# PSUM as one ring of four two-bank tiles, and attention visits of three score tiles

## The chip, the cores and the metric

The kernel runs on one core of a Trainium2 chip. The metric is the device time of the program in microseconds; the median of several runs is given, and every ratio is against runs of the kernel before made on the same chip in the same rounds. All runs of this study are of the same (fast) state. A profile is of one execution only, and its first 110 us vary most from run to run. The span of a profile is 1.8 us shorter than the time of the same execution (446.4 against 448.2 us for the kernel before).

## The reference

Sigmoid attention over 8 batches, 12 heads, 448 positions and 64 channels, followed by a gated feed-forward block (3584 tokens, 768 to 1536 and back).

```python
def _attn_ref(q, k, v):
    S = q.shape[2]
    scores = (1.0 / np.sqrt(q.shape[-1])) * np.matmul(q, k.transpose(0, 1, 3, 2)) - np.log(S)
    return np.matmul(1.0 / (1.0 + np.exp(-scores)), v).astype(np.float32)

def _moe_ref(x, w_gate, w_val, w_out):
    g = x @ w_gate
    silu = g * (1.0 / (1.0 + np.exp(-g)))
    return (silu * (x @ w_val) @ w_out).astype(np.float32)
# x = attention output as (B*S, H*D) = (3584, 768); w_gate, w_val 768 x 1536; w_out 1536 x 768
```

## The kernel before

TensorE, the matmul engine, carries the kernel, and its program order is fixed by hand. Feed-forward units stand one after the other (a unit is a gate and a value product for 128 hidden columns; an output unit is 128 output rows in two halves), and *visits* of attention are put between them. A visit computes score tiles (four matmuls on 64 x 64 quarters of the array side by side, 128 x 896 in PSUM, the buffer that matmuls write into), and some visits also hold the PV product (28 such matmuls) of a group of four heads. The feed-forward matmuls use the array as one piece of 128 x 128, so every visit changes the shape of the array and changes it back. ScalarE turns a score tile into probabilities (the sigmoid), and VectorE does most of the other reading of PSUM. The first batch's attention runs alone at the start.

The kernel divides PSUM by banks (in this code, stretches of 512 FP32 columns) and uses eight. The scores have two tiles of two banks, and all else shares four tiles of one bank. A tile is handed out again when its readers are done. Which tile is next, and all waits, follow from the order in which the kernel issues its instructions.

```python
psA = ctx.enter_context(tc.tile_pool(name="psA", bufs=2, space=bass.MemoryType.PSUM))   # scores
psG = ctx.enter_context(tc.tile_pool(name="psG", bufs=4, space=bass.MemoryType.PSUM))   # all else
# ...
def trans_pe(n, which):                      # q or k, transposed on TensorE
    t = q16.pop((n, which))
    ps = psG.tile([128, C, 128], BF16, tag="G", name="ps_tr")
    for c in range(C):
        nc.tensor.transpose(out=ps[:, c, :], in_=t[:, c].rearrange("p h d -> p (h d)"), identity=idn)
    d = qkT.tile([128, C, 128], BF16, tag=f"T{which}", name=f"T{which}_{n}")
    nc.vector.tensor_copy(out=d, in_=ps)
# ...
def ffn1(b, f, gate):                        # one half-unit: gate or value
    ps = psG.tile([128, S], FP32, tag="G", name="ps_g" if gate else "ps_vl")
    # ... six matmuls into ps
    if gate:
        s16 = tmp.tile([128, S], FP16, tag="s16", name="s16")
        nc.scalar.activation(out=s16, in_=ps, func=SIGM)
        t1 = tmp.tile([128, S], FP16, tag="t1", name="t1")
        nc.vector.tensor_tensor(out=t1, in0=ps, in1=s16, op=MULT)
    # ... value: hT = ps * HSC * t1 on VectorE

def ffn2(b, m, half):                        # one output half-unit
    # ...
    o = psG.tile([128, hw], FP32, tag="G", name="ps_o")
    # ... twelve matmuls into o, then one VectorE read of o into osb
# ...
visits = [tiles[i:i + 2] for i in range(0, len(tiles), 2)]

def attn_step(group, pvs):
    scs = [(n, c, qk_tile(n, c)) for n, c in group]
    for n in pvs:
        pv(n)
    for n, c, sc in scs:
        sig_tile(n, c, sc)
```

Of the kernel before, what the change touches and what calls it, by code (L numbers as in the profile page):

```python
# [17 lines left out]
def kernel(  # L18
# [28 lines left out]
    psA = ctx.enter_context(tc.tile_pool(name="psA", bufs=2, space=bass.MemoryType.PSUM))  # L47
    psG = ctx.enter_context(tc.tile_pool(name="psG", bufs=4, space=bass.MemoryType.PSUM))
# [67 lines left out]
    def trans_pe(n, which):  # L116
        t = q16.pop((n, which))
        ps = psG.tile([128, C, 128], BF16, tag="G", name="ps_tr")
        for c in range(C):
            nc.tensor.transpose(  # L120
                out=ps[:, c, :], in_=t[:, c].rearrange("p h d -> p (h d)"), identity=idn
            )
        d = qkT.tile([128, C, 128], BF16, tag=f"T{which}", name=f"T{which}_{n}")
        nc.vector.tensor_copy(out=d, in_=ps)  # L124
        qT[(n, which)] = d
# [5 lines left out]
    def qk_tile(n, c):  # L131
        sc = psA.tile([128, 2, 512], FP32, tag="A", name="ps_sc")
# [18 lines left out]
    def pv(n):  # L151
        b, j = divmod(n, NJ)
        P = [psG.tile([128, S], FP32, tag="G", name=f"ps_pv{w}") for w in range(2)]
        vt = v16.pop(n)
        for c in range(C):
            pt = pts.pop((n, c))
            for h2 in range(2):
                for w in range(2):
                    r = slice(w * 64, w * 64 + 64)
                    nc.tensor.matmul(  # L160
                        out=P[w][h2 * 64:(h2 + 1) * 64, :],
# [5 lines left out]
        for h2 in range(2):  # L167
            x = xtp.tile([128, S], FP16, tag="xT", name=f"xT_{b}_{2 * j + h2}")
            for w in range(2):
                nc.vector.tensor_copy(  # L170
                    out=x[w * 64:(w + 1) * 64, :], in_=P[w][h2 * 64:(h2 + 1) * 64, :]
                )
            xT[(b, 2 * j + h2)] = x
# [5 lines left out]
    gcur = {}  # L179

    def ffn1(b, f, gate):
        ps = psG.tile([128, S], FP32, tag="G", name="ps_g" if gate else "ps_vl")
        w = (wg16 if gate else wv16)[f // FW]
        cs = slice((f % FW) * 128, (f % FW) * 128 + 128)
        for pr in range(NP):
            nc.tensor.matmul(  # L186
                out=ps, lhsT=w[:, pr, cs], rhs=xT[(b, pr)], start=(pr == 0), stop=(pr == NP - 1)
            )
        if gate:
            s16 = tmp.tile([128, S], FP16, tag="s16", name="s16")  # L190
            nc.scalar.activation(out=s16, in_=ps, func=SIGM)  # L191
            t1 = tmp.tile([128, S], FP16, tag="t1", name="t1")
            nc.vector.tensor_tensor(out=t1, in0=ps, in1=s16, op=MULT)  # L193
            gcur[0] = t1
        else:
            if b % 2 == 0:
                hT[(b // 2, f)] = htp.tile([128, 2, S], FP16, tag="hT", name=f"hT_{b // 2}_{f}")
            nc.vector.scalar_tensor_tensor(  # L198
                out=hT[(b // 2, f)][:, b % 2, :], in0=ps, scalar=HSC, in1=gcur[0], op0=MULT, op1=MULT
            )  # L200

    osb_cur = {}

    def ffn2(b, m, half):
        hw = DM // 2
        if half == 0:
            osb_cur[0] = osp.tile([128, DM], FP32, tag="osb", name="osb")
        osb = osb_cur[0]
        o = psG.tile([128, hw], FP32, tag="G", name="ps_o")
        for f in range(NF):  # L210
            h = hT[(b // 2, f)].rearrange("p b s -> p (b s)")
            lhsT = h[:, m * 128:(m + 1) * 128]
            nc.tensor.matmul(  # L213
                out=o,
                lhsT=lhsT,
                rhs=wo16[f // FW][:, f % FW, half * hw:(half + 1) * hw],
                start=(f == 0),
                stop=(f == NF - 1),
            )
        nc.vector.tensor_scalar(  # L220
# [175 lines left out]
```

## Time and profile before

| | before |
|---|---|
| time | 449.93 us, median of 3 runs (449.58 to 449.96) |
| span of the profile | 446.4 us |
| TensorE busy | 420.9 us, 94% |
| VectorE, ScalarE busy | 49%, 47% |

This is the waits view of the kernel before, TensorE alone (who waited for whom: us in total, times, longest):

```profile
PE ps_sc L137 <- ACT pt L148: 7.2, 10, 2.1
PE ps_tr L120 <- DVE c L108: 4.7, 1, 4.7
PE ps_tr L120 <- ACT c L106: 1.8, 1, 1.8
PE ps_sc L137 <- DVE T L124: 1.6, 2, 0.9
PE ps_g L186 <- DVE xT L170: 1.4, 2, 0.9
...
```

All but 0.5 us of this lies in the first 40 us. After that a single gate product waits, 0.5 us for its input xT.

### The profile page before, as it was taken

The numbers are of one execution on the slowest core, as the hardware profiler recorded it, in microseconds if no ns is written. First come the engines' busy times: TensorE is split into PE (matmuls) and PEld (weight loads), VectorE is DVE, ScalarE is ACT, GpSimd is POOL, SyncE is SP. The second block draws the span as 40 slices with busy tenths as digits, with TensorE's granted clock in tenths as the row PEclk, the third lists the DMA queues.
The fourth block names the chain that finished last, engine by engine and source line by source line (L and its number), as shares of the span: only waits on it lengthen the run. The fifth ranks groups of instructions, "written<-read, shape, count | busy, mean of one in ns | idle before, by whom it ended". The sixth has DMA issues, their size and how long they took to land.

```text
span 446.4 us, 7870 instructions
## 1 busy us (share of the span) xinstructions
PE 420.9 (94%) x3252; PEld 212.2 (48%) x3252; DVE 220.1 (49%) x360; ACT 210.9 (47%) x267; POOL 100.7 (23%) x142
## 2 busy tenths in 40 slices
PE   2678999999999999999999999999999999999992
PEld 1344444444555444444555444444555545555661
DVE  1265665466334456556424546646524446555231
ACT  3887675655533655565444464565444441221000
POOL 1764140220234512000324612200021100000221
PEclk9899999999999999999999999999999999999998
DMA  8999999994284986500278694220033300000242
GB/s 264 332 286 286 182 249 196 232 280 149 58 249 94 262 248 167 164 1 1 50 222 231 135 302 134 42 42 3 0 82 87 79 4 1 1 1 0 72 106 70
DMA packets 63587, 59.88 MB, mean 134 GB/s; under 512 B 35648, under 2 KB 61760, under 8 KB 63552
## 3 DMA queue, kind: packets, MB, share of 16 engines
q1 hardware_dynamic: 52992, 41.30, 34.8%
q0 software_dynamic: 10560, 18.09, 19.3%
q8 instruction: 25, 0.41, 0.4%
q14 instruction: 10, 0.08, 0.1%
HBM read 47.19 MB, written 11.01 MB: 130 GB/s over the span
## 4 chain that ended last, share of the span: by engine, by line
PE 92%; ACT 2%; DMA 2%; DVE 1%; issue 1%; POOL 0%; SPq 0%; POOLq 0%; ACTq 0%
PE ps_o L213 25%; PE ps_vl L186 25%; PE ps_g L186 25%; PE ps_sc L137 9%; PE ps_pv L160 7%; ACT pt L148 2%; DMA st<-in_q_dram 2%; PE ps_tr L120 1%; DVE xT L170 1%; SPq L88 0%; POOL c L108 0%; DVE osb L220 0%; POOL out_dram L228 0%; POOLq L391 0%; ACTq L148 0%
## 5 line engine op out<-in xcount | busy, mean ns | idle before, releaser
L148 ACT ACTIVATE pt<-ps_sc,sb_t 128x896 f16<-128x896 f32 x168 | 159.6, 1005 | 88.5 <-PE ps_sc L137 88.5
L186 PE MATMUL ps_g<-xT,wg 128*128 128x448 f16 x576 | 125.4, 353 | 1.5 <-DVE xT L170 1.4
L186 PE MATMUL ps_vl<-xT,wv 128*128 128x448 f16 x576 | 124.9, 353 | 0.0
L213 PE MATMUL ps_o<-wo,hT 128*128 128x384 f16 x672 | 113.5, 326 | 0.0
L193 DVE TENSOR_TENSOR t<-ps_g,s 128x448 f16<-128x448 f32 x96 | 59.9, 624 | 84.7 <-ACT s L191 84.1
L191 ACT ACTIVATE s<-ps_g 128x448 f16<-128x448 f32 x96 | 52.2, 544 | 103.2 <-PE ps_g L186 103.2
L213 PEld LDWEIGHTS <-hT 128*128 128x128 f16 x672 | 64.0, 98 | 48.6 <-issue 7.9
L186 PEld LDWEIGHTS <-wv 128*128 128x128 f16 x576 | 54.3, 98 | 58.6 <-issue 10.7
L186 PEld LDWEIGHTS <-wg 128*128 128x128 f16 x576 | 54.1, 98 | 57.0 <-issue 9.7
L228 POOL DMA_DIRECT2D out_dram<-osb x56 | 29.3, 528 | 211.2 <-DVE osb L220 211.0
L170 DVE CAST xT<-ps_pv 64x448 f16<-64x448 f32 x96 | 59.7, 622 | 30.8 <-PE ps_pv L160 29.4
L198 DVE SCALAR_TENSOR_TENSOR hT<-ps_vl,t 128x448 f16<-128x448 f32 x96 | 60.0, 625 | 16.6 <-PE ps_vl L186 8.5
L220 DVE TENSOR_SCALAR osb<-ps_o 128x384 f32<-128x384 f32 x56 | 31.2, 558 | 74.6 <-PE ps_o L213 74.4
L137 PE MATMUL ps_sc<-T,T 64*64 64x448 bf16 x672 | 51.1, 370 | 8.8 <-ACT pt L148 7.2
L108 POOL CAST c<-st 128x896 bf16<-128x896 f32 x43 | 39.7, 939 | 54.7 <-DMA st<-in_q_dram 30.3
L108 POOL CAST v<-st 128x896 f16<-128x896 f32 x24 | 22.6, 942 | 72.8 <-PE ps_pv L160 52.9
L160 PE MATMUL ps_pv<-pt,v 64*64 64x448 f16 x672 | 37.5, 359 | 0.3 <-ACT pt L148 0.3
L137 PEld LDWEIGHTS <-T 64*64 64x64 bf16 x672 | 13.7, 106 | 39.7 <-issue 37.1
L160 PEld LDWEIGHTS <-v 64*64 64x64 f16 x672 | 20.8, 109 | 12.8 <-issue 0.9
L120 PE MATMUL ps_tr<-idn,c 128*128 128x128 bf16 x84 | 7.3, 250 | 6.5 <-DVE c L108 4.7
L120 PEld LDWEIGHTS <-c 128*128 128x128 bf16 x84 | 5.9, 113 | 8.8 <-DVE c L108 4.7
L124 DVE COPY T<-ps_tr 128x896 bf16<-128x896 bf16 x12 | 7.1, 620 | 5.4 <-PE ps_tr L120 5.2
(14 smaller groups left out, 17.2 us busy)
## 6 DMA issues: line engine op xcount, KB each, us to landing
st<-in_q_dram SPq DMA_DIRECT2D x24, 448.0 KB, 4.5
st<-in_k_dram SPq DMA_DIRECT2D x24, 448.0 KB, 5.9
st<-in_v_dram SPq DMA_DIRECT2D x24, 448.0 KB, 7.3
out_dram<-osb POOLq DMA_DIRECT2D x56, 192.0 KB, 3.1
wg<-in_moe_w_gate_dram POOLq DMA_DIRECT2D x4, 576.0 KB, 24.8
wv<-in_moe_w_val_dram POOLq DMA_DIRECT2D x4, 576.0 KB, 29.7
wo<-in_moe_w_out_dram POOLq DMA_DIRECT2D x4, 576.0 KB, 35.4
T<-c SPq DMA_TRANSPOSE x36, 3.2
```

Of the source, the lines that this page charges most:

```text
L108: eng.tensor_copy(out=o, in_=i)
L137: nc.tensor.matmul(out=sc[w * 64:(w + 1) * 64, h2, :S], lhsT=kt[r, c, w * 64:(w + 1) * 64], rhs=qt[r, :, w * 64:(w + 1) * 64], start=True, ...
L148: nc.scalar.activation(out=pt, in_=sc[:, :, :S], func=SIGM, bias=sb_t, scale=qkscale)
L160: nc.tensor.matmul(out=P[w][h2 * 64:(h2 + 1) * 64, :], lhsT=vt[r, h2, c * D:(c + 1) * D], rhs=pt[r, h2, :], start=(c == 0), stop=(c == C - 1),
L170: nc.vector.tensor_copy(out=x[w * 64:(w + 1) * 64, :], in_=P[w][h2 * 64:(h2 + 1) * 64, :])
L186: nc.tensor.matmul(out=ps, lhsT=w[:, pr, cs], rhs=xT[(b, pr)], start=(pr == 0), stop=(pr == NP - 1))
L191: nc.scalar.activation(out=s16, in_=ps, func=SIGM)
L193: nc.vector.tensor_tensor(out=t1, in0=ps, in1=s16, op=MULT)
L198: nc.vector.scalar_tensor_tensor(out=hT[(b // 2, f)][:, b % 2, :], in0=ps, scalar=HSC, in1=gcur[0], op0=MULT, op1=MULT)
L213: nc.tensor.matmul(out=o, lhsT=lhsT, rhs=wo16[f // FW][:, f % FW, half * hw:(half + 1) * hw], start=(f == 0), stop=(f == NF - 1),)
L220: nc.vector.tensor_scalar(out=osb[:, half * hw:(half + 1) * hw], in0=o, scalar1=HREC, scalar2=None, op0=MULT)
L228: nc.gpsimd.dma_start(out=dst, in_=osb[i * 64:(i + 1) * 64, :])
```

## The change

The intent: one ring of four two-bank tiles for all stages gives the first batch four score tiles instead of two, and makes room for visits of three score tiles, so that the array changes its shape less often. Gate and value of a unit, the two output halves, the two PV tiles, and the transposes of q and k each become the two halves of one tile. The core of the diff (PV likewise, and the transposes of a later group are issued one step earlier; cuts marked):

```diff
-    psA = ctx.enter_context(tc.tile_pool(name="psA", bufs=2, space=bass.MemoryType.PSUM))
-    psG = ctx.enter_context(tc.tile_pool(name="psG", bufs=4, space=bass.MemoryType.PSUM))
+    psD = ctx.enter_context(tc.tile_pool(name="psD", bufs=4, space=bass.MemoryType.PSUM))
 ...
+    def trans_pe(n):
+        ps = psD.tile([128, 2, 8, 128], BF16, tag="D", name="ps_tr")
+        for which in range(2):
+            t = q16.pop((n, which))
+            for c in range(C):
+                nc.tensor.transpose(out=ps[:, which, c, :], ...)
+            d = qkT.tile([128, C, 128], BF16, tag=f"T{which}", name=f"T{which}_{n}")
+            nc.vector.tensor_copy(out=d, in_=ps[:, which, :C, :])
 ...
+    def ffn1(b, f):
+        D = psD.tile([128, 2, 512], FP32, tag="D", name="ps_gv")
+        for i, w16 in enumerate((wg16, wv16)):
+            ...  # six matmuls into D[:, i, :S]
+        nc.scalar.activation(out=s16, in_=D[:, 0, :S], func=SIGM)
+        ...  # t1 from D[:, 0], hT from D[:, 1] on VectorE
+    def ffn2(pb, m):
+        D = psD.tile([128, 2, 512], FP32, tag="D", name="ps_o")
+        for half in range(2):
+            ...  # twelve matmuls into D[:, half, :hw]
+            nc.vector.tensor_scalar(out=osb[:, half * hw:(half + 1) * hw], in0=D[:, half, :hw], ...)
 ...
-    visits = [tiles[i:i + 2] for i in range(0, len(tiles), 2)]
+    visits = [tiles[i:i + 3] for i in range(0, len(tiles), 3)]
 ...
-        scs = [(n, c, qk_tile(n, c)) for n, c in group]
+        scs = [(n, c, qk_tile(n, c)) for n, c in group[:2]]
         for n in pvs:
             pv(n)
+        scs += [(n, c, qk_tile(n, c)) for n, c in group[2:]]
```

More of the change, by code (lines that the diff above doesn't have):

```diff
@@ L114, in trans_dma @@
         qT[(n, which)] = d
-    def trans_pe(n, which):
-        t = q16.pop((n, which))
-        ps = psG.tile([128, C, 128], BF16, tag="G", name="ps_tr")
-        for c in range(C):
-            nc.tensor.transpose(
-                out=ps[:, c, :], in_=t[:, c].rearrange("p h d -> p (h d)"), identity=idn
-            )
-        d = qkT.tile([128, C, 128], BF16, tag=f"T{which}", name=f"T{which}_{n}")
-        nc.vector.tensor_copy(out=d, in_=ps)
-        qT[(n, which)] = d
+    def trans_pe(n):
[3 more added lines that the diff above has]
+            for c in range(C):
+                nc.tensor.transpose(
+                    out=ps[:, which, c, :], in_=t[:, c].rearrange("p h d -> p (h d)"), identity=idn
+                )
+            d = qkT.tile([128, C, 128], BF16, tag=f"T{which}", name=f"T{which}_{n}")
+            nc.vector.tensor_copy(out=d, in_=ps[:, which, :C, :])
+            qT[(n, which)] = d
     pts = {}
@@ L131, in qk_tile @@
     def qk_tile(n, c):
-        sc = psA.tile([128, 2, 512], FP32, tag="A", name="ps_sc")
+        sc = psD.tile([128, 2, 512], FP32, tag="D", name="ps_sc")
         qt, kt = qT[(n, 0)], qT[(n, 1)]
@@ L152, in pv @@
         b, j = divmod(n, NJ)
-        P = [psG.tile([128, S], FP32, tag="G", name=f"ps_pv{w}") for w in range(2)]
+        P = psD.tile([128, 2, 512], FP32, tag="D", name="ps_pv")
         vt = v16.pop(n)
@@ L160, in pv @@
                     nc.tensor.matmul(
-                        out=P[w][h2 * 64:(h2 + 1) * 64, :],
+                        out=P[h2 * 64:(h2 + 1) * 64, w, :S],
                         lhsT=vt[r, h2, c * D:(c + 1) * D],
@@ L170, in pv @@
                 nc.vector.tensor_copy(
-                    out=x[w * 64:(w + 1) * 64, :], in_=P[w][h2 * 64:(h2 + 1) * 64, :]
+                    out=x[w * 64:(w + 1) * 64, :], in_=P[h2 * 64:(h2 + 1) * 64, w, :S]
                 )
@@ L178 @@
     hT = {}
-    gcur = {}
-    def ffn1(b, f, gate):
-        ps = psG.tile([128, S], FP32, tag="G", name="ps_g" if gate else "ps_vl")
-        w = (wg16 if gate else wv16)[f // FW]
+    def ffn1(b, f):
+        D = psD.tile([128, 2, 512], FP32, tag="D", name="ps_gv")
         cs = slice((f % FW) * 128, (f % FW) * 128 + 128)
-        for pr in range(NP):
-            nc.tensor.matmul(
-                out=ps, lhsT=w[:, pr, cs], rhs=xT[(b, pr)], start=(pr == 0), stop=(pr == NP - 1)
-            )
-        if gate:
-            s16 = tmp.tile([128, S], FP16, tag="s16", name="s16")
-            nc.scalar.activation(out=s16, in_=ps, func=SIGM)
-            t1 = tmp.tile([128, S], FP16, tag="t1", name="t1")
-            nc.vector.tensor_tensor(out=t1, in0=ps, in1=s16, op=MULT)
-            gcur[0] = t1
-        else:
-            if b % 2 == 0:
-                hT[(b // 2, f)] = htp.tile([128, 2, S], FP16, tag="hT", name=f"hT_{b // 2}_{f}")
-            nc.vector.scalar_tensor_tensor(
-                out=hT[(b // 2, f)][:, b % 2, :], in0=ps, scalar=HSC, in1=gcur[0], op0=MULT, op1=MULT
-            )
@@ L202 @@
-    osb_cur = {}
-    def ffn2(b, m, half):
-        hw = DM // 2
-        if half == 0:
-            osb_cur[0] = osp.tile([128, DM], FP32, tag="osb", name="osb")
-        osb = osb_cur[0]
-        o = psG.tile([128, hw], FP32, tag="G", name="ps_o")
-        for f in range(NF):
-            h = hT[(b // 2, f)].rearrange("p b s -> p (b s)")
-            lhsT = h[:, m * 128:(m + 1) * 128]
-            nc.tensor.matmul(
-                out=o,
-                lhsT=lhsT,
-                rhs=wo16[f // FW][:, f % FW, half * hw:(half + 1) * hw],
-                start=(f == 0),
-                stop=(f == NF - 1),
-            )
-        nc.vector.tensor_scalar(
-            out=osb[:, half * hw:(half + 1) * hw], in0=o, scalar1=HREC, scalar2=None, op0=MULT
-        )
-        if half == 1:
-            for i in range(2):
-                bb, c = divmod(2 * m + i, C)
-                bb += b - b % 2
-                dst = out[bb * S:(bb + 1) * S, :].rearrange("(p c) n -> c p n", c=C)[c]
-                nc.gpsimd.dma_start(out=dst, in_=osb[i * 64:(i + 1) * 64, :])
@@ L231 @@
-    FU1, FU2 = 1.13, 1.95
+        for i, w16 in enumerate((wg16, wv16)):
+            for pr in range(NP):
+                nc.tensor.matmul(
+                    out=D[:, i, :S], lhsT=w16[f // FW][:, pr, cs], rhs=xT[(b, pr)],
+                    start=(pr == 0), stop=(pr == NP - 1),
+                )
+        s16 = tmp.tile([128, S], FP16, tag="s16", name="s16")
+        nc.scalar.activation(out=s16, in_=D[:, 0, :S], func=SIGM)
+        t1 = tmp.tile([128, S], FP16, tag="t1", name="t1")
+        nc.vector.tensor_tensor(out=t1, in0=D[:, 0, :S], in1=s16, op=MULT)
@@ new lines, in ffn1 @@
+        if b % 2 == 0:
+            hT[(b // 2, f)] = htp.tile([128, 2, S], FP16, tag="hT", name=f"hT_{b // 2}_{f}")
+        nc.vector.scalar_tensor_tensor(
+            out=hT[(b // 2, f)][:, b % 2, :], in0=D[:, 1, :S], scalar=HSC, in1=t1, op0=MULT, op1=MULT
+        )
+    def ffn2(pb, m):
+        hw = DM // 2
+        osb = osp.tile([128, DM], FP32, tag="osb", name="osb")
+        D = psD.tile([128, 2, 512], FP32, tag="D", name="ps_o")
+        for half in range(2):
+            for f in range(NF):
+                h = hT[(pb, f)].rearrange("p b s -> p (b s)")
+                nc.tensor.matmul(
+                    out=D[:, half, :hw],
+                    lhsT=h[:, m * 128:(m + 1) * 128],
+                    rhs=wo16[f // FW][:, f % FW, half * hw:(half + 1) * hw],
+                    start=(f == 0),
+                    stop=(f == NF - 1),
+                )
+            nc.vector.tensor_scalar(
+                out=osb[:, half * hw:(half + 1) * hw], in0=D[:, half, :hw], scalar1=HREC, scalar2=None, op0=MULT
+            )
+        for i in range(2):
+            bb, c = divmod(2 * m + i, C)
+            bb += 2 * pb
+            dst = out[bb * S:(bb + 1) * S, :].rearrange("(p c) n -> c p n", c=C)[c]
+            nc.gpsimd.dma_start(out=dst, in_=osb[i * 64:(i + 1) * 64, :])
@@ L232 @@
+    FU1, FU2 = 2.26, 3.9
     units = []
@@ L238 @@
             for f in range(NF):
-                units.append((FU1, ("g", b, f)))
-                units.append((FU1, ("v", b, f)))
-                tt += 2 * FU1
+                units.append((FU1, ffn1, (b, f)))
+                tt += FU1
             f1_end[b] = tt
         for m in range(7):
-            for half in range(2):
-                units.append((FU2, ("o", 2 * pb + (m > 2), m, half)))
-                tt += FU2
+            units.append((FU2, ffn2, (pb, m)))
+            tt += FU2
     FIRST, PER = f1_end[0] - 5.0, 38.5
     tiles = [(n, c) for n in range(NJ, NQ) for c in range(C)]
-    visits = [tiles[i:i + 2] for i in range(0, len(tiles), 2)]
+    visits = [tiles[i:i + 3] for i in range(0, len(tiles), 3)]
     vtime = []
@@ L282 @@
     cast(0, 2, nc.gpsimd)
-    trans_pe(0, 0)
-    trans_pe(0, 1)
+    trans_pe(0)
     cast(1, 1, nc.vector)
@@ L293 @@
         if (n, c) == (0, 3):
-            trans_pe(1, 0)
-            trans_pe(1, 1)
+            trans_pe(1)
             cast(2, 0, nc.gpsimd)
@@ L301 @@
         if (n, c) == (1, 3):
-            trans_pe(2, 0)
-            trans_pe(2, 1)
+            trans_pe(2)
             load3(4)
@@ L310 @@
         if (n, c) == (2, 3):
-            trans_pe(3, 0)
-            trans_pe(3, 1)
+            trans_pe(3)
             load3(5)
@@ L326 @@
     pend = []
-    for dur, u in units:
+    for dur, fn, args in units:
         while vi < len(visits) and tcur >= vtime[vi]:
@@ L351 @@
                             w_load(*wl.pop(0))
-                if c == 5 and n + 1 < NPE:
-                    trans_pe(n + 1, 0)
-                    trans_pe(n + 1, 1)
-        if pend and (u[0] == "g" and u[2] == 0 and (u[1], NP - 1) not in xT or vi == len(visits) and tcur >= vtime[-1] + 4.0):
+                if c == 4 and n + 1 < NPE:
+                    trans_pe(n + 1)
+        if pend and (
+            fn is ffn1 and args[1] == 0 and (args[0], NP - 1) not in xT
+            or vi == len(visits) and tcur >= vtime[-1] + 4.0
+        ):
             for n in pend:
@@ L358 @@
             pend = []
-        if u[0] == "g":
-            ffn1(u[1], u[2], True)
-        elif u[0] == "v":
-            ffn1(u[1], u[2], False)
-        else:
-            ffn2(*u[1:])
+        fn(*args)
         tcur += dur
```

## The prediction

> **What bounds the kernel now.** I read the page first: busy shares, then the 40 slices, then the chain that ended last.
>
> ```profile
> PE 420.9 (94%) x3252; PEld 212.2 (48%) x3252; DVE 220.1 (49%) x360; ACT 210.9 (47%) x267; POOL 100.7 (23%) x142
> ...
> PE   2678999999999999999999999999999999999992
> ...
> PE 92%; ACT 2%; DMA 2%; DVE 1%; issue 1%; POOL 0%; SPq 0%; POOLq 0%; ACTq 0%
> ```
>
> The reader is to see one engine. TensorE carries 92% of the chain and is full in every slice but the first four and the last; VectorE and ScalarE are half busy. The windows view, split at 34.9 us (first feed-forward matmul), 368.6 (last attention) and 410.7 (last output products), puts the idle at the two ends:
>
> ```profile
> 0.00:34.90 34.90, 19.32 (x233) 10.72 (x233) 12.87 (x21) 23.14 (x25) 18.51 (x27) 0.95 1.04 294
> 34.90:368.60 333.70, 332.16 (x2635) 163.41 (x2632) 173.89 (x285) 177.99 (x225) 74.86 (x101) 1.00 0.59 140
> ```
>
> From 34.9 to 368.6 the busy time is 332.16 of 333.70 us, so no more than 1.5 us of waiting can be removed there. But a busy matmul row isn't a row at its best speed, so I went to the timeline, for one attention visit (two score tiles) between two feed-forward half-units:
>
> ```profile
> 198.03 1.30 PE L186 MATMUL ps_vl<-xT,wv 128*128 128x448 f16 x6
> ...
> 199.25 0.14 PEld L137 LDWEIGHTS <-T 64*64 64x64 bf16 x8 [0.37 <-issue]
> 199.25 0.57 PE L137 MATMUL ps_sc<-T,T 64*64 64x448 bf16 x8
> ...
> 199.69 1.91 ACT L148 ACTIVATE pt<-ps_sc,sb_t 128x896 f16<-128x896 f32 x2 [0.92 <-PE ps_sc L137]
> 199.76 0.87 PEld L186 LDWEIGHTS <-wg 128*128 128x128 f16 x6 [0.36 <-issue]
> 199.76 1.31 PE L186 MATMUL ps_g<-xT,wg 128*128 128x448 f16 x6
> ...
> 200.91 1.30 PE L186 MATMUL ps_vl<-xT,wv 128*128 128x448 f16 x6
> ```
>
> The number after the start is the group's length. Read starts only. Undisturbed half-units start 1.135 us apart (at 385.62, 386.76, 387.89, 389.03 in the tail). Here two of them with a visit between take 200.91 - 198.03 = 2.88 us, so the visit costs 2.88 - 2.27 = 0.61 us. Its eight matmuls run four abreast at 0.189 us per tile, 0.38 us; the other **0.23 us is the change of array shape, there and back**. A visit between output units agrees: 24 matmuls start at 121.49, the next 24 at 126.00, and 4.51 - 24 x 0.1625 = 0.61.
>
> **What the Trainium skill says.** "TensorEngine Tiling (Array Packing)", Key Properties: "Changing tiling mode (not just tile) drains the TensorE". The trace agrees: the weight loads idle 0.37 and 0.36 us at the two changes, 0.23 us net. "TensorE: Matmul & The Clock Gate", section on 56 against 53.3 ns: columns over 2.4 GHz plus about 2.5 ns per matmul; for 448 columns 189 ns, and the trace has 1.135 / 6 = 189 ns, so nothing else is left inside a stretch of one shape. "Perfetto Trace Analysis", Tensor Engine Instruction: the end of a matmul is estimated; the rows overlap (1.30 us long, 1.135 apart), which is why I use starts. "TensorEngine Tiling", PSUM Bottleneck: tiled matmuls outrun the emptying of PSUM; here one score tile is 0.19 us on TensorE and 0.95 on ScalarE. This decides the case.
>
> **The change part by part.** No arithmetic is removed: the built programs have the same matmuls, sigmoids and copies.
>
> (1) Fewer visits. The 147 score tiles after the first batch come in 49 groups of three, not 74 of two. Counting changes between 64-row and 128-row shapes in the two built instruction orders gives 156 before and 106 after: 25 round trips x 0.23 = **-5.9 us**. A PV product already sat inside a visit; putting it between the second and third tile costs nothing.
>
> (2) The start. Before, two score buffers tie TensorE to ScalarE in the first batch, and the transposes queue behind a score tile waiting for its buffer:
>
> ```profile
> 13.05 0.59 PE L137 MATMUL ps_sc<-T,T 64*64 64x448 bf16 x4 [0.31 <-ACT pt L148]
> ...
> 13.57 1.41 PEld L120 LDWEIGHTS <-c 128*128 128x128 bf16 x14 [0.38 <-issue]
> ...
> 15.82 5.50 ACT L148 ACTIVATE pt<-ps_sc,sb_t 128x896 f16<-128x896 f32 x6 [1.02 <-PE ps_sc L137]
> ...
> 16.88 0.38 PE L137 MATMUL ps_sc<-T,T 64*64 64x448 bf16 x4 [0.82 <-ACT pt L148]
> ...
> 23.09 1.01 ACT L148 ACTIVATE pt<-ps_sc,sb_t 128x896 f16<-128x896 f32 x1 [1.76 <-PE ps_sc L137]
> ```
>
> Here ScalarE, which needs 21 x 0.92 = 19.4 us for the batch, idles 1.02, then 1.76, then 0.2 three times: 3.4 us between 11.1 and 34.2. With four buffers TensorE runs four tiles ahead; walking the new order through with these durations leaves about 1 us of gaps. The first feed-forward unit then ends about 2.4 us earlier. The gate and value weights limit this: transfers saturate the engines there (share 1.04). I take **-2 us**.
>
> (3) The new wait. A feed-forward unit now needs a two-bank tile from the same four. I looked up in the built program which tile each one gets and what it waits for. It is not a strict rotation: after a visit of three score tiles without PV, the next feed-forward unit gets the tile of the **first score of that very visit**, and its first matmul waits for that sigmoid. ScalarE starts it 0.44 us after the visit's first weight load (199.25 to 199.69). A matmul that reuses a tile follows 1.06 us after the sigmoid's start (15.82 to 16.88 in the fence above). So the unit starts 0.44 + 1.06 = 1.50 us after the visit began. Without the wait it would at 0.51 (199.25 to 199.76) + 0.19 for the third tile = 0.70. The wait costs 0.80 us, all on TensorE; a drain it covers is already in the 0.70. In the program 18 feed-forward units have this wait, after the first (which waits for xT anyway), and one transpose group: 19 x 0.80 = **+15.2 us**.
>
> (4) Visits with PV don't pay: PV puts 1.32 us before the third tile, at 1.72 us, when the first sigmoid (1.50) is done. Output units after three scores get the previous output unit's tile; VectorE empties it 0.67 us after the visit's start (125.49 to 125.60 + 0.56), so with the signal's passage they lose some 0.05 us, nine times: +0.4 us. Gate, value and output halves paired in one tile change no duration; the last 20 units and 7 output units run as before.
>
> Sum: -5.9 - 2 + 15.2 + 0.4 = +7.7 us, on 449.93: **457.6 us**, 1.7% slower.
>
> **The rivals.** (a) The tile is free in time, so only (1) and (2) remain: 449.93 - 7.9 = 442.0. For it: four tiles hold more scores than two, and a strict rotation would give the unit the tile of the unit before the visit. Against it: the built program names the sigmoid. Even in strict rotation the wait would not vanish: VectorE's last read of the value half runs from 199.53 to 200.15, 0.90 us after the visit's start, and reuse about 0.06 later, at 0.96 against 0.70.
> (b) ScalarE becomes the bound: three sigmoids in a row (2.9 us) delay the gate's sigmoid, VectorE follows late, and the later reuses of a tile wait too. For it: VectorE already waits for that sigmoid.
>
> ```profile
> DVE t L193 <- ACT s L191: 84.1, 80, 2.2
> ```
>
> Against it: the sigmoids end 3.3 us after the visit began, when the delayed unit has just had its gate product (1.50 + 1.13 = 2.63); the unit is empty by about 5.2 us, and the next visit comes at 6 us or later. If some of these waits bite, 460 to 463.
> (c) Weights arrive later than the earlier start needs, so (2) gives nothing: 459.6. The value weights of the first, second, third and fourth groups land at about 31, 45, 56 and 67 us, worked out from the sorted times from issue to landing; before, the last is used at 68.2, so the margin is 1 us. By my walk the new kernel uses it near 67.9, as its first three waits have eaten the gain.
>
> **Range and chances.** Count and size of the wait are each known to about a tenth (15.2 gives 13 to 16.5). The start may give 0 to 2.5 us. Rival (b) adds a tail above. Range 452.5 to 461.0. Slower by over 2% means over 458.9, half a standard deviation above my value: 0.28. Faster by over 2% (under 440.9) would need rival (a) and more: 0.02. Within 2%: 0.70.
>
> **What would show it.** In the new waits view: TensorE's feed-forward matmuls waiting for the sigmoid of scores (PE ps_gv from ACT pt), near 19 times, 0.6 to 0.9 us each, 12 to 16 us in total, where before it has none after 40 us. In the timeline, a three-score visit without PV followed 1.50 us after its first weight load by the gate matmul, and one with PV not. The first batch's sigmoids end near 31.5 us instead of 34.2. TensorE's busy time falls by about 6 us while the span grows; its total idle rises from 25.5 us to about 39. ScalarE, VectorE busy unchanged. The prediction is wrong if those waits are missing or under 0.4 us (then 442 to 449), or if VectorE's reads of PSUM hold up TensorE as well (then above 461).

## More of the kernel before

From the last stage, with output units alone, the matmuls and two of VectorE's reads (one per half; the read between them is left out):

```profile
424.73 13.33 PE L213 MATMUL ps_o<-wo,hT 128*128 128x384 f16 x81
...
426.39 0.56 DVE L220 TENSOR_SCALAR osb<-ps_o 128x384 f32<-128x384 f32 x1 [1.39 <-PE ps_o L213]
...
430.29 0.56 DVE L220 TENSOR_SCALAR osb<-ps_o 128x384 f32<-128x384 f32 x1 [1.39 <-PE ps_o L213]
```

The matmuls run on without a stop, and two halves take 430.29 - 426.39 = 3.90 us.

## The result

The changed kernel takes **491.52 us** (median of 4 runs, 490.21 to 492.97) against 449.75 us: 9.5% slower (ratio 1.0947, 95% interval 1.089 to 1.1005). Ratios here are the mean time of one kernel's runs over the mean of the other's of the same rounds, so not quite the ratio of the medians. The time lies 30 us above the range that was predicted.

The page of the changed kernel, the busy shares, the row of TensorE in 40 slices and the chain by engine:

```profile
PE 425.0 (87%) x3252; PEld 220.2 (45%) x3252; DVE 221.3 (45%) x360; ACT 208.7 (43%) x267; POOL 100.3 (21%) x142
...
PE   3777789899888999899888999999988899999882
...
PE 78%; DVE 9%; ACT 7%; DMA 2%; issue 2%; SPq 0%; POOL 0%; POOLq 0%; DVEq 0%; ACTq 0%
```

The same work is there on each engine, but TensorE's row now has 7 and 8 in many slices, and VectorE and ScalarE hold 16% of the chain. The waits view says for what TensorE waited:

```profile
PE ps_o L208 <- DVE osb L215: 19.8, 28, 1.0
PE ps_gv L187 <- ACT pt L150: 15.9, 19, 0.8
PE ps_tr L122 <- DVE T L126: 8.4, 5, 2.6
```

The second line is the wait of the prediction's step (3), foretold as 19 times and 15.2 us. (Its 19 include the first unit, which the prediction had left out; after 46 us it is 18 gate products, 15.1 us, and one group of transposes, 0.8 us.) The first and the third were not foretold at all.

A table of stages shows where the 42 us lie. The borders are the first matmul of each stage in the timelines: F are feed-forward units (two batches each), O are output units with visits between them, and the last column is the seven output units at the end, without any attention.

| us | start | F1 | O1 | F2 | O2 | F3 | O3 | F4 | O4 and end |
|---|---|---|---|---|---|---|---|---|---|
| before | 34.9 | 75.7 | 34.8 | 68.9 | 34.2 | 70.2 | 34.2 | 57.7 | 35.8 |
| after | 39.6 | 82.5 | 40.0 | 73.1 | 40.3 | 73.5 | 40.3 | 57.7 | 41.5 |

The output stages together lose 23.0 us (from unrounded starts), the feed-forward stages F1 to F3 14.3, the start 4.7. Most of F4 has no visits (before, the last attention ends at 368.6 us and F4 at 410.6), and it loses nothing.

**Output units.** O4 is the plainest place, for nothing but output units runs there, and the prediction said that it would stay as it was. From the timeline of the changed kernel (start, length of the group, engine, operation; in brackets the idle time before it and what ended it):

```profile
468.57 4.06 PE L208 MATMUL ps_o<-wo,hT 128*128 128x384 f16 x24 [0.65 <-DVE osb L215]
...
470.72 0.56 DVE L215 TENSOR_SCALAR osb<-ps_o 128x384 f32<-128x384 f32 x1 [2.20 <-PE ps_o L208]
...
472.67 0.56 DVE L215 TENSOR_SCALAR osb<-ps_o 128x384 f32<-128x384 f32 x1 [1.39 <-PE ps_o L208]
473.28 4.06 PE L208 MATMUL ps_o<-wo,hT 128*128 128x384 f16 x24 [0.65 <-DVE osb L215]
```

The period of a unit is 473.28 - 468.57 = 4.71 us; before, two halves took 3.90. The later of the two reads shown ends (472.67 + 0.56 = 473.23), and 0.05 us later the matmuls go on. Each group of 24 between two such waits is the *second* half of one unit and the *first* half of the next: in the built program, and in the trace for all 28 units, this wait stands on the thirteenth matmul of the unit, and it is for the read of the *first* half of the same tile. The two halves are different banks, but the program keeps its dependences for the tile as a whole, so a matmul into one half has to wait until the read of the other half, issued before it, is over.

**Transposes.** The same happens at the start. From the timeline of the changed kernel:

```profile
20.30 2.53 DVE L172 CAST xT<-ps_pv 64x448 f16<-64x448 f32 x4 [4.22 <-PE ps_pv L162]
...
20.55 0.93 PE L122 MATMUL ps_tr<-idn,c 128*128 128x128 bf16 x7
...
22.86 0.62 DVE L126 COPY T<-ps_tr 128x896 bf16<-128x896 bf16 x1
23.53 0.91 PE L122 MATMUL ps_tr<-idn,c 128*128 128x128 bf16 x7 [2.05 <-DVE T L126]
...
25.07 5.49 ACT L150 ACTIVATE pt<-ps_sc,sb_t 128x896 f16<-128x896 f32 x6 [3.34 <-PE ps_sc L139]
```

The transposes of q are done at 21.5; those of k start only at 23.53, after the copy of q out of the same tile, which itself stands behind four PV copies on VectorE. The next scores stand behind the transposes in TensorE's order, so ScalarE idles 3.34 us. This turned the expected gain of the start into a loss (e2 below tests it).

**Gate and value.** The tile-wide dependence also delays the gate's sigmoid until the value product is in. In the changed kernel:

```profile
299.52 1.30 PE L187 MATMUL ps_gv<-xT,wg 128*128 128x448 f16 x6
...
300.66 1.30 PE L187 MATMUL ps_gv<-xT,wv 128*128 128x448 f16 x6
...
301.99 0.54 ACT L192 ACTIVATE s<-ps_gv 128x448 f16<-128x448 f32 x1 [1.73 <-PE ps_gv L187]
302.43 2.79 ACT L150 ACTIVATE pt<-ps_sc,sb_t 128x896 f16<-128x896 f32 x3
...
303.48 1.29 PE L187 MATMUL ps_gv<-xT,wg 128*128 128x448 f16 x6 [0.84 <-ACT pt L150]
```

The sigmoid starts 1.33 us after the value product began. Before, it started 0.20 us after that (value at 198.03, sigmoid at 198.23). By itself this seems to cost little (no run parts it from the rest): it makes the first score sigmoid of a visit some 0.1 us later (0.55 us after the visit's start at 301.88, not 0.44), so the next gate product starts 1.60 us after the visit began and not 1.50.

### The profile page after: what moved, and what is told of

Its sections match the earlier page's. It is cut to its first block, busy times and chain, and to the rows that moved or that the text cites. A ratio compares the mean times of both kernels' runs of the same rounds, so it can differ in the third digit from the quotient of the medians.

```text
span 488.4 us, 7775 instructions
## 1 busy us (share of the span) xinstructions
PE 425.0 (87%) x3252; PEld 220.2 (45%) x3252; DVE 221.3 (45%) x360; ACT 208.7 (43%) x267; POOL 100.3 (21%) x142
## 4 chain that ended last, share of the span: by engine, by line
PE 78%; DVE 9%; ACT 7%; DMA 2%; issue 2%; SPq 0%; POOL 0%; POOLq 0%; DVEq 0%; ACTq 0%
PE ps_gv L187 45%; PE ps_o L208 22%; PE ps_pv L162 6%; ACT pt L150 5%; PE ps_sc L139 4%; DVE xT L172 4%; DVE osb L215 3%; ACT s L192 2%; DMA st<-in_k_dram 2%; PE ps_tr L122 1%; DVE T L126 1%; SPq L89 0%; DVE t L194 0%; DVE hT L197 0%; DVE c L109 0%
## 5 line engine op out<-in xcount | busy, mean ns | idle before, releaser
L150 ACT ACTIVATE pt<-ps_sc,sb_t 128x896 f16<-128x896 f32 x168 | 156.6, 1008 | 89.7 <-PE ps_sc L139 89.7
L187 PE MATMUL ps_gv<-xT,wg 128*128 128x448 f16 x576 | 124.9, 352 | 16.1 <-ACT pt L150 15.9
L208 PE MATMUL ps_o<-wo,hT 128*128 128x384 f16 x672 | 116.3, 326 | 19.8 <-DVE osb L215 19.8
L187 PE MATMUL ps_gv<-xT,wv 128*128 128x448 f16 x576 | 124.6, 352 | 0.0
L194 DVE TENSOR_TENSOR t<-ps_gv,s 128x448 f16<-128x448 f32 x96 | 60.0, 625 | 124.5 <-ACT s L192 124.4
L192 ACT ACTIVATE s<-ps_gv 128x448 f16<-128x448 f32 x96 | 52.1, 543 | 142.6 <-PE ps_gv L187 142.6
L187 PEld LDWEIGHTS <-wv 128*128 128x128 f16 x576 | 56.4, 98 | 53.0 <-issue 0.4
L197 DVE SCALAR_TENSOR_TENSOR hT<-ps_gv,t 128x448 f16<-128x448 f32 x96 | 59.9, 624 | 3.3
L139 PEld LDWEIGHTS <-T 64*64 64x64 bf16 x672 | 16.9, 110 | 26.4 <-issue 20.9
L162 PEld LDWEIGHTS <-v 64*64 64x64 f16 x672 | 21.0, 111 | 15.9 <-issue 3.7
L122 PE MATMUL ps_tr<-idn,c 128*128 128x128 bf16 x84 | 9.2, 270 | 16.2 <-DVE T L126 8.4
```

The source lines that it names most:

```text
L139: nc.tensor.matmul(out=sc[w * 64:(w + 1) * 64, h2, :S], lhsT=kt[r, c, w * 64:(w + 1) * 64], rhs=qt[r, :, w * 64:(w + 1) * 64], start=True, ...
L150: nc.scalar.activation(out=pt, in_=sc[:, :, :S], func=SIGM, bias=sb_t, scale=qkscale)
L162: nc.tensor.matmul(out=P[h2 * 64:(h2 + 1) * 64, w, :S], lhsT=vt[r, h2, c * D:(c + 1) * D], rhs=pt[r, h2, :], start=(c == 0), stop=(c == C ...
L187: nc.tensor.matmul(out=D[:, i, :S], lhsT=w16[f // FW][:, pr, cs], rhs=xT[(b, pr)], start=(pr == 0), stop=(pr == NP - 1),)
L192: nc.scalar.activation(out=s16, in_=D[:, 0, :S], func=SIGM)
L194: nc.vector.tensor_tensor(out=t1, in0=D[:, 0, :S], in1=s16, op=MULT)
```

## The experiments

Theory A: the loss that was not foretold is the waiting of one half of a tile for the read of its other half. Rival B: VectorE is late by its own load, or its reads of PSUM get in the way of the matmuls. Beside these, the terms of the prediction were tested: the visits alone, the ring alone, and a cheaper kind of visit. All runs gave correct results. In the short diffs "-" is the kernel named first.

### e1: both output halves before both reads

```diff
                     stop=(f == NF - 1),
                 )
-            nc.vector.tensor_scalar(out=osb[...], in0=D[:, half, :hw], ...)
+        for half in range(2):
+            nc.vector.tensor_scalar(out=osb[...], in0=D[:, half, :hw], ...)
```

> The changed kernel, but each output unit issues both halves' matmuls before both VectorE reads; same instructions, same PSUM tiles. Theory A (the wait of a half on VectorE's read of the other half of its own two-bank tile is the lost time): in the tail an output unit falls from 4.71 us to about 3.90, the waits of PE ps_o for DVE osb (19.8 us, 28 times) all but vanish; 28 x 0.81 = 22.7 us and some 2.6 us where PV copies stood in front of the read come back, but where an output unit takes the tile of the unit just before a visit (8 times) it now waits for two reads, 1.28 us after the visit's start against 0.70: +4.6. About 471 us. Rival B (VectorE is late by its own load, or PSUM reads slow the matmuls): the same reads of the same length remain, so the waits stay or move to the next unit, and the time stays within 5 us of 491.5.

Measured: 470.39 us, ratio 1.0465 (1.0403 to 1.0526). O1 to O3 fall to 35.4 us each and O4 to 36.3, and the wait of ps_o for osb falls from 19.8 us (28 times) to 3.4 us (8 times), the eight units that take the tile of the unit just before the visit. The same reads on the same VectorE cost TensorE 16 us less when only their place in the order changes, which speaks against B.

### e2: e1, and both transposes before both copies

```diff
-            d = qkT.tile([128, C, 128], BF16, tag=f"T{which}", name=f"T{which}_{n}")
-            nc.vector.tensor_copy(out=d, in_=ps[:, which, :C, :])
+        for which in range(2):
+            d = qkT.tile([128, C, 128], BF16, tag=f"T{which}", name=f"T{which}_{n}")
+            nc.vector.tensor_copy(out=d, in_=ps[:, which, :C, :])
```

> As e1_o_order, and the transposes of k are issued before the copy of q out of the same tile. Theory A: in the first batch the scores queue behind the second half of a transpose tile, which waits for the copy of the first half, which stands behind four PV copies on VectorE; without that, ScalarE's gaps of 3.34 and 2.78 us shrink to under 1 us each, and two later waits of 0.7 us go: 5 to 6.5 us less than e1, about 465 us, and the first feed-forward unit ends at 36 to 37 us instead of 42.2. Rival (the first batch is bound by the arrival of data): no more than 1 us less than e1.

Measured: 460.08 us, ratio 1.0276 (1.0183 to 1.0369). The step from e1 is 10.3 us, more than the 5 to 6.5 expected: the start falls from 39.6 to 32.6 us, and F1 from 83.8 to 78.8. Two groups of transposes lie in F1; in e1 they waited 0.7 us (behind the copy of q alone) and 2.6 us (behind PV copies as well). The wait of ps_tr for T is gone. Not all of the step need be the order's: in e1's profile the granted clock was 0.57 from 30 to 40 us and 0.83 from 60 to 70, in e2's 1.00 in both, and after the 2.6 us wait some of e1's feed-forward matmuls start 0.37 us apart and not 0.19, some 1.3 us in all. (The changed kernel has the same 2.60 us wait without such a slow stretch, so the wait alone does not explain it.) The first feed-forward unit now starts 2.3 us earlier than in the kernel before, in line with the gain that step (2) of the prediction had counted on. These are single profiles; but over the six runs of the ring with this order mended the unit starts at 31.6 to 33.9 us, and over the eight with the old pools at 33.6 to 37.2.

### e9: each output half in a tile of its own, order untouched

This parts the tile from the order. The program's order on each engine is that of the changed kernel.

```diff
-        D = psD.tile([128, 2, 512], FP32, tag="D", name="ps_o")
         for half in range(2):
+            D = psD.tile([128, 2, 512], FP32, tag="D", name="ps_o")
```

> The changed kernel with one edit: each half of an output unit takes a tile of its own from the ring (half of it unused). The order of the instructions on every engine stays that of the changed kernel. Theory A (the wait comes from both halves lying in one tile, whose dependences are kept for the tile as a whole): the second half no longer waits for the read of the first; an output unit in the tail takes 3.90 us instead of 4.71, 28 x 0.81 + 2.6 = 25 us less, about 466 us; unlike e1 no unit has to wait for two reads. Rival B (the order of matmul, read, matmul, read, or VectorE's load, makes the wait): 491 us as the changed kernel.

Measured: 466.96 us, ratio 1.0415 (1.0389 to 1.044); expected 466. The wait of ps_o for osb is no longer in the waits view, whose first line is now:

```profile
PE ps_gv L187 <- ACT pt L150: 15.5, 19, 0.8
```

O1 to O3 take 34.0 us each (34.2 to 34.8 before, with more visits), and in O4 the reads, which now follow every half without stopping anything, come 1.95 us apart (from the timeline of e9, a stretch of O4):

```profile
444.83 13.16 PE L208 MATMUL ps_o<-wo,hT 128*128 128x384 f16 x80
...
446.33 0.56 DVE L215 TENSOR_SCALAR osb<-ps_o 128x384 f32<-128x384 f32 x1 [1.39 <-PE ps_o L208]
...
448.29 0.56 DVE L215 TENSOR_SCALAR osb<-ps_o 128x384 f32<-128x384 f32 x1 [1.39 <-PE ps_o L208]
```

With each read running while the next half is being written, in the order of the changed kernel, and no loss, B falls. The output halves cost 491.5 - 467.0 = 24.5 us; the four O stages of the two profiles give 24.3.

### e13: both waits taken away, nothing else

e9 and the transposes of e2 together: what is left should be just what the prediction reckoned with.

> The changed kernel with both omitted waits taken away and nothing else: each output half in a tile of its own (as e9, order unchanged) and both transposes issued before both copies (as in e2). What is left is what my prediction reckoned with: -5.9 us of switches, -2 of the start, +15 to 16 for the sigmoid waits. If the two omitted waits are the whole error, the time is 456 to 458 us (ratio about 1.017), the first feed-forward unit starts at 32 to 33 us, and output stages take about 34.0 us. If something else of the ring costs too, 461 us or more.

Measured: 458.26 us, ratio 1.0187 (1.0145 to 1.0228). The prediction, 457.6 us, is a ratio of 1.017. So the two waits that were left out are as large as its whole error, within the spread of these runs (455.5 to 462.1). The profile fell on the slowest of the four; it shows the sigmoid waits as foretold, and weights that came late, the prediction's rival (c):

```profile
PE ps_gv L188 <- ACT pt L151: 15.7, 19, 0.8
...
PE ps_gv L188 <- DMA wv<-in_moe_w_val_dram: 4.4, 3, 2.1
```

The first feed-forward unit starts at 31.6 us, but F1 takes 86.6. Beside the 4.4 us for weights, F1 lost some 2.9 us between 70 and 80 us to matmuls at a lower granted clock (0.66 in that stretch). That the median lies so near the prediction may therefore be luck in part: an earlier start and late weights offset each other.

### e6: the pools of before, with visits of three

```diff
-    visits = [tiles[i:i + 2] for i in range(0, len(tiles), 2)]
+    visits = [tiles[i:i + 3] for i in range(0, len(tiles), 3)]
 # and the third score after PV, transposes one step earlier, as in the change
```

> The kernel before with its own two PSUM pools, only with visits of three scores (PV before the third) as in the change. Switches between matrix shapes fall from 156 to 106, worth -5.8 us, and with PV inside nothing waits. But in the visits without PV the third score takes the buffer of the first and waits for its sigmoid at 1.5 us after the visit's start instead of 0.4: 28 x 1.1 = +31. About 475 us. If the saving of a round trip is not 0.23 us or the wait is hidden elsewhere, the time will lie well off this.

Measured: 473.68 us, ratio 1.0549 (1.0489 to 1.0609); expected 475. Larger visits by themselves are a loss, as the third score has to wait for the first sigmoid. From its timeline, a visit without PV and one with:

```profile
158.39 0.57 PE L137 MATMUL ps_sc<-T,T 64*64 64x448 bf16 x8
159.95 0.38 PE L137 MATMUL ps_sc<-T,T 64*64 64x448 bf16 x4 [0.98 <-ACT pt L148]
...
166.04 0.57 PE L137 MATMUL ps_sc<-T,T 64*64 64x448 bf16 x8
166.44 1.49 PE L160 MATMUL ps_pv<-pt,v 64*64 64x448 f16 x28
167.77 0.36 PE L137 MATMUL ps_sc<-T,T 64*64 64x448 bf16 x4
```

The third score starts 1.56 us after the visit's first matmul where nothing stands before it; with PV it starts at 1.73 us and waits for nothing.

### e3: the ring alone (mended order, visits of two)

```diff
-    visits = [tiles[i:i + 3] for i in range(0, len(tiles), 3)]      # e2
+    visits = [tiles[i:i + 2] for i in range(0, len(tiles), 2)]
```

> Ring of four two-bank tiles with both order mendings (as e2), but visits of two scores as in the kernel before: the ring alone, without the larger visits. In the built program no unit after a visit without PV takes a tile of that visit or of the unit just before it. Theory A: the waits of ps_gv for ACT pt (15.9 us in the changed kernel) are gone, the 24 round trips of array shape come back (+5.5 us): about 449 us, within 1% of before. Rival (a two-bank ring costs in itself, since a tile comes free only when both halves are read and the gate's sigmoid starts only after the value product): 455 us or more.

Measured: 452.79 us, ratio 1.0083 (1.0049 to 1.0117), 3.8 us above what was expected. The sigmoid waits are gone, and F2, O2, F3 and O3 take 68.9, 34.2, 70.2 and 34.2 us, to the tenth as before: with a mended order the ring costs nothing there. The rest is in the first stretch: the feed-forward starts at 31.7 us but F1 takes 80.4, with 2.6 us of waiting for value weights and 2.4 for xT. So the earlier start is given back in F1, in part to weights that aren't there yet.

### e4: the pools of before, a third score only beside PV

```diff
-    visits = [tiles[i:i + 2] for i in range(0, len(tiles), 2)]
+    visits, i, has_pv = [], 0, False
+    while i < len(tiles):
+        visits.append(tiles[i:i + (3 if has_pv else 2)])
+        i += len(visits[-1])
+        has_pv = any(c == C - 1 for _, c in visits[-1])
 # and the third score after PV; transposes one step earlier
```

> The kernel before with its own pools, and a third score only in the visits that carry a PV product, where PV (1.32 us) covers the wait for the first sigmoid (third score wanted at 1.72 us, sigmoid over at 1.50). 136 switches of shape instead of 156: 10 round trips x 0.23 = -2.3 us: 447.4 us, 0.5% faster than before. Rival (a switch's cost is hidden or belongs to something else): no difference.

Measured: 447.83 us, ratio 0.9966 (0.9938 to 0.9995); expected 447.4. F2 and F3 fall from 68.9 and 70.2 to 68.4 and 67.8 us, while O3, into which some attention moved, rises from 34.2 to 36.1; from O1 to the end the kernel is 2.0 us shorter. This measures the change of shape by itself. F2 holds 30 score tiles and four PV products in both kernels and no wait in either, but 26 changes of shape instead of 30: 68.91 - 68.44 = 0.47 us for two round trips, 0.235 each. But F1 rises from 75.7 to 79.4, and a wait stands there that before did not have:

```profile
PE ps_vl L186 <- DMA wv<-in_moe_w_val_dram: 4.0, 2, 2.8
```

### e5: the mended ring with the visits of e4

> Ring with both order mendings and the mixed visits of e4: 134 switches, no wait for a sigmoid after a visit without PV; the third score takes the tile of the unit just before the visit 7 times, wanted at 1.72 and free at about 2.0 us: +2 us at most. Against e3 -10 x 0.23 = -2.3 us, +1 to 2: about 448 us. If the start is quicker by 2 us with four score tiles (what my prediction held), 446.

Measured: 449.62 us, ratio 1.0017 (0.9987 to 1.0047). The gain on e3 is 3.2 us; F1 takes 79.6 us here too. It equals the kernel before, no more.

### e7 and e8: load of the sixth q, k, v group put off

A first attempt to get the value weights in time, on e4 and on e5: the load of group 5 is moved from the first batch to the first visit after it.

> e4 (pools of before, a third score only beside PV) with the load of the sixth q, k, v group put off from the first batch to the first visit after it, so that the gate and value weights share the transfers with less. In e4 TensorE waited 4.0 us for value weights (at 58.1 and 71.1 us) where before had no such wait. If the weights are late because the q, k, v loads take the transfers: that wait falls under 1.5 us and the time to 444 to 446 us. Rival: the weights are paced by their own queue, or the sixth group is now late itself: no gain, or a loss of 1 to 3 us.

> e5 (ring with both mendings, mixed visits) with the same later load. In e5 the value weights cost 1.2 us and the first two batches' feed-forward stage took 79.6 us against 75.7 before. If the loads of q, k, v are what delays it: 446 to 448 us; rival as for e7: no gain.

Measured: 447.91 us (ratio 0.9993, 0.9963 to 1.0023) and 448.61 us (1.0009, 0.9984 to 1.0034). No gain that can be seen; in e7 the wait for the weights is still 3.7 us. The guess that the load of this group keeps the weights away fails.

### e10 and e11: gate, value and output weights in two groups of six

> e4 (pools of before, a third score only beside PV) with gate, value and output weights loaded in two groups of six columns of tiles instead of four of three: rows twice as long, the same bytes. In e4 TensorE waited 4.0 us for value weights, e7 showed that putting off q, k, v does not help, so their own queue paces them. If longer rows carry more bytes in the same turn: the wait falls under 1 us, 443 to 445 us, over 1% faster than before. Rival: the first group is twice as large and now holds up the first feed-forward unit: 449 us or more.

> The kernel before with the same two weight groups of six and nothing else: the control for e10. Before has no wait for weights in its profile, so no gain is expected: 449 us; a loss if the first group comes late.

Measured: 454.54 us (ratio 1.0118, 1.0089 to 1.0146) and 456.76 us (1.0167, 1.0134 to 1.02). Both are misses: e10 came out where its rival had put it (449 us or more), but not for the reason given there (the first unit starts at 34.4 us, in e4 at 33.9), and e11 is 7.8 us over what was expected. In e10 no weight is waited for, but one score waits for its transposed q and k:

```profile
PE ps_sc L137 <- DMA T<-c: 8.4, 1, 8.4
```

(e11 waits 3.3 us for the same.) The transfer engines are busy throughout: in e10's windows of the first 90 us their share is 0.92 to 1.41. That what is given to one transfer is taken from another fits this, but was not shown.

### e12 and e15: the output weights asked for later

```diff
-                        if wl:
+                        if wl and n >= 6:
```

e12 is e4 with this edit; e15, the control, is the kernel before with it.

> e4 with the output weights asked for some 40 us later (they are needed at 113 us, asked for at 38 and 45). If they share the queue's turns with the last value weights, the 4.0 us wait shrinks and the time is 444 to 446 us; if the queue serves in order, nothing changes: 447.8.

> The kernel before with the later output weights alone, the control of e12. Before waits for no weights in its profile, so no gain: ratio 1.000 within 0.3%; then e12's gain is that of the mixed visits, set free by the later output weights.

Measured: e12 takes **445.72 us** (ratio 0.993, 0.9901 to 0.996), the fastest. The wait for value weights is down from 4.0 to 0.7 us and F1 from 79.4 to 76.5 us. The control, 448.36 us (ratio 0.9987, 0.9963 to 1.0012), shows no difference that can be told. So the reading is that the gain belongs to the mixed visits, once the output weights, which are needed only at about 110 us, are asked for at 69 and 76 us instead of 38 and 45 and no longer run beside the value weights. The profiles say so; by the times alone e12 (0.993) and e4 (0.9966) have intervals that overlap. How the transfers share the engines was not measured.

### e14: the ring at its best

e13 with the visits of e4 and the later output weights.

> The ring at its best by what is known: e13 with a third score only beside PV and the output weights asked for 40 us later. Against e5 (449.6) the wait for value weights (1.2 us) should go, and the two-read waits with it: 446 to 447 us. If four two-bank tiles are as good as the pools of before, it equals e12 (445.7, ratio 0.993); if the shared ring still costs by slower emptying, it stays 1 to 3 us behind.

Measured: 447.15 us, ratio 0.9968 (0.9937 to 0.9998). The mended ring is as good as the old pools within the spread of the runs, but not better: it reaches the feed-forward 1.7 us earlier than e12 (32.3 against 34.0 us) and loses 1.9 us in F1 (78.4 against 76.5), both from single profiles.

The stages of the kernels that carry the argument (profiled runs, us):

| | start | F1 | O1 | F2 | O2 | F3 | O3 | F4 | O4 and end |
|---|---|---|---|---|---|---|---|---|---|
| after | 39.6 | 82.5 | 40.0 | 73.1 | 40.3 | 73.5 | 40.3 | 57.7 | 41.5 |
| e9 own tiles for output halves | 40.5 | 83.8 | 34.0 | 73.1 | 34.0 | 73.5 | 34.0 | 57.7 | 35.8 |
| e2 both orders mended | 32.6 | 78.8 | 35.3 | 73.1 | 35.4 | 73.5 | 35.4 | 57.7 | 36.3 |
| e3 ring, visits of two | 31.7 | 80.4 | 35.2 | 68.9 | 34.2 | 70.2 | 34.2 | 57.7 | 36.3 |
| e6 old pools, visits of three | 37.2 | 81.5 | 37.3 | 74.6 | 37.3 | 74.8 | 37.3 | 58.0 | 35.8 |
| e12 old pools, mixed visits | 34.0 | 76.5 | 34.0 | 68.4 | 34.6 | 67.8 | 36.1 | 57.1 | 35.8 |

## Why the prediction was wrong

"Within 2%" had a chance of 0.70 and "slower" 0.28; the time came out 9.5% slower, 30 us above the upper end of the range. Point by point:

- **The step that failed** is in (4): "Gate, value and output halves paired in one tile change no duration; the last 20 units and 7 output units run as before." The last 20 units did, the 7 output units did not. A tile of two banks is one thing to the program that guards it. A half that is read makes the next matmul into the other half wait. For the output units this cost 24.5 us (e9), where nothing was reckoned (the 0.4 us in step (4) is for another wait, after visits).
- **Step (2), the start**, fell by the same oversight. It was -2 us and came out at +4.7. The walk through the new order had the transposes of q and k follow each other without a pause. Taking the wait away brings the first feed-forward unit 2.3 us before that of the kernel before (e2), so the mechanism was there. Start and F1 together, the transposes' order is worth 10.3 us by the medians (e1 to e2), with the reserve on the clock made there.
- **The sum closes to about the spread of the runs.** Changed kernel, less the output halves, less the transposes: 491.5 - 24.5 - 10.3 = 456.7 us; e13, which takes away just these two, measured 458.3; the prediction without them was 457.6.
- **Step (3), the new wait for the visit's own first sigmoid**, held: 18 gate products and one group of transposes waited 15.9 us, against 19 and 15.2. Its cost was a little larger. F2 has the same scores and PV products before and after, 4.5 round trips fewer and six waits more, and takes 4.2 us longer: (4.2 + 4.5 x 0.23) / 6 = 0.87 us for each wait, not 0.80. The gate product starts 1.60 us after the visit began instead of the 1.50 reckoned, as the gate's sigmoid, itself held back by the tile-wide dependence, stands ahead of the score's.
- **Step (1), 0.23 us per round trip**, held: F2 of e4 against F2 before measures 0.235 (see e4). The counts of changes of shape in the traces are those of the prediction, 156 and 106. That e4's time came out as expected (447.8 against 447.4) is no further proof, since its F1 lost 4.0 us to weights. A slip: 25 x 0.23 is 5.75 us, not 5.9, which would put the sum at 457.8.
- **Rival (a)** fell: the wait is there. **Rival (b)** did not show: after the first 46 us, TensorE waits for ScalarE in just these visits (18 times before a gate product, once before a transpose). **Rival (c)**, late weights, came true in the mended versions (e3, e13), where it ate much of the earlier start. "TensorE's busy time falls by about 6 us" failed: it rose from 420.9 to 425.0 us, and idle time went to 63.4 us, not 39. With both waits mended it falls, to 416.6 (e2) and 418.1 (e13).
- **What should have been seen before the run.** The list of waits in the built program has a wait for VectorE on the thirteenth matmul of every output unit and on the eighth of every transpose group. I took it for the guard of the second bank's previous user, and looked up only the first matmul of each tile. Following that one number to its instruction would have named the read of the first half, and a term for 28 such waits would have been in the sum (22.7 us, with the 0.81 us that each was then measured to cost).

What stays open: why the value weights land when they do, and why some profiles show a stretch of lower granted clock in the first 80 us and others, with the same waits, don't. e7, e10 and e12 show what moves the weights and what doesn't, not the rule.

## What to carry to other kernels

If two results share a tile, write both before reading either, or give each a tile of its own; writing, reading and writing again in turn made the matmuls here wait for every read, although the halves lay in different banks. Look up every wait in the built program, those in the middle of a tile too, and name the instruction at its other end. And put extra work into a stage only where something covers the wait that it brings: a third score tile pays beside a PV product of 1.3 us and loses elsewhere.

## What the Trainium skill lacked or had wrong

- "PSUM — Partial Sum Buffer", section PSUM bank collisions, gives the rule "Semaphore-guard PSUM by **bank × quadrant** (by bank is the simple version), not by address." The runs agree as far as they go: in e9 one half is read while the next, in another bank, is written, at 1.95 us per half, with correct results. No run tried two accesses to one bank. What the page doesn't say is that a program may guard by whole tile, and what that costs when the tile spans two banks: 0.81 us for each output unit here (4.71 against 3.90), 24.5 us in all (e9).
- "TensorEngine Tiling (Array Packing)", Key Properties, says that a change of mode drains the array but gives no figure. Here a round trip between 128 x 128 and 64 x 64 costs 0.23 us, worked out from the timeline of the kernel before, and again from F2 of e4.
- No page that I read gives the time from the end of a read to the matmul that takes over its tile: here 0.05 us (VectorE's read ends at 473.23, the matmul starts at 473.28).
